# Attention with pooled keys and a phase-mixing layer: GpSimd's queue issues weight loads and a part of the other transfers

## The chip, the cores and the metric

One core of a Trainium2 chip runs the whole program. The time is device microseconds of one execution. TensorE (PE) multiplies, VectorE (DVE), ScalarE (ACT) and GpSimd (POOL) do the elementwise work, and SyncE (SP) does nothing but issue transfers between the memory of the chip and the core's on-chip memory. Every engine works through its own list of instructions in order and waits for the others by semaphores. The kernel before takes 245.79 us, the median of three runs (245.34 to 246.45).

## What is computed

```python
def _attn_ref(q, k, v):                       # (8, 8, 576, 64) each
    q_d, k_d, v_d = means over 4 neighbouring positions
    out_d = softmax(q_d @ k_d.T / 8) @ v_d
    out_up = np.repeat(out_d, 4, axis=2)
    mask = np.abs(pos[:, None] - pos[None, :]) < 4
    out_local = softmax(where(mask, q @ k.T / 8, -1e9)) @ v
    return out_up + out_local

def _moe_ref(x, w_theta, w_tok_r, w_tok_i, w_ch):   # x (8, 576, 512)
    theta = x @ w_theta
    zr, zi = x * np.cos(theta), x * np.sin(theta)
    y = einsum('ts,bsd->btd', w_tok_r, zr) + einsum('ts,bsd->btd', w_tok_i, zi)
    u = x + y
    return u + np.maximum(u @ w_ch, 0.0)
```

All inputs and the output are float32. The heads of the attention's result, side by side, are the 512 columns of x. w_theta and w_ch are 512 x 512, the two token weights 576 x 576.

## The kernel before, in words

The work goes batch by batch, 0 to 7, with several batches in flight. For a batch, 13 items are loaded in float32 into staging buffers (`st`, 15 of them, used in turn): four of k, four of q (each 128 rows of 2,304 bytes, one transfer) and five of v (two transfers each, L220, with a run of 256 bytes for each position and head). A cast to bfloat16 follows on POOL, ACT or DVE (`cast`, L226). PE turns k and q into columns (L300) through PSUM, copies bring them to kT and qT, DVE sums groups of four keys (L317) and POOL, for all batches but the first, groups of four queries (L334, L335). PE computes the pooled scores (L382, L394), the pooled v (L348, L350) and the pooled result (L414, L420), and the local scores (L468) and outputs (L500). The two parts meet in xT (L540, L552).

The second layer takes the phases (L567, L585), sine and cosine on ACT (L574, L575, L592, L593), the products z on DVE (L634), the mix over positions (L654, against WT), the sum u (L663), the channel product (L693, L699) and the relu with the residual (L706), whose left side comes turned by transposing transfers (L670). Stores go out at L719 and L725.

The weights come in 20 pieces, WITEMS: four of w_theta (128 x 512), twelve of the token weights (96 x 576; three pieces of r, three of i for the first half of the positions, then the same for the second), four of w_ch. Each goes over a staging buffer (`weight_loads`, L249) and a cast (`weight_casts`, L258) to wth, w_tm or wch; w_tm is then turned by PE (L276) into WT. The two halves of WT are read by different mixes: batch 0 takes its four mixes of the first half before those of the second.

What stands in which place is written out. ORDER is a string in which each letter is one step of a sequence (the table at L747): L one load, l one weight load, c one weight cast, C one cast of an input, J one mix, D one store, Y the two stores of a tail, 1 and 2 a load of an ACT table for sine or exponential, and so on. The kernel takes the letters one by one, and `pin` (L733) ties every instruction to the one before it on the same engine, so that the string fixes the order on each engine, SP's list of transfers too. BANKS gives the PSUM bank of each step, ENGINES the engine (v DVE, a ACT, p POOL) of each copy. In the kernel before, all 205 loads and stores and all 52 transposing transfers are issued by SP; POOL issues none.

Of the kernel before, what the change touches and what calls it, by code (L numbers as in the profile page):

```python
# [14 lines left out]
P = 128  # L15
# [3 lines left out]
D = 64  # L19
DM = 512  # L20
# [14 lines left out]
WR = 9  # L35
PG = CH // 4
KP = 32
HALF = 64
# [3 lines left out]
OC = 96  # L42
# [3 lines left out]
def kernel(  # L46
# [11 lines left out]
    nc = tc.nc  # L58
# [5 lines left out]


    ORDER = (
        "kLCLkLkCk2ACLCkaAkLCkLLCLLLCdlCaAAaaSkLkklSLLedSLLePsLCmsCOOmLkLsPpCCLlCookipULOuuxxLoCCOCNiioCCcN1l"
        "nLinTAAnnQcaClcaATLCmqtacCtOAHdTaoiSlhLXLdtyTeleLLsSPtsHPlCCmOpcLpSCsmloCTiOCcUlOtocuXuHoiOhcCiVhxom"
        "xNyiCGccHLALLganLVvVnLZVvLzNVlvVlXClvvLCnVnyCAQlvValhCACCveVLqXcvTtTcaAvlTtyaOoticHdTS2STsLsdecJHcJV"
        "LhcXttJvVhyVCVCvvvlXVyvLGVCVLVLgJLvZCvLVvvPjjjpCmJUjLuuHOxjoCiCOPJpxomiLNCXnHjLJnChNjAcLCJnyhCnLXjyT"  # L70
        "azCQLAAJCqaAlTLlLdJtLaSaLCjtOsoOiceJjjoCSLmLCJcTiClOtjsLCSCUHCRJeCuoiTTudRsCxLLjACtLJhaLtALJaGjmgOOj"
        "xPoJRoCiHiCcSpPjedCCXRKsLpmbyhKNZACnXbLHyaCLHhnXKyCLNhLLAbXzfKLCamUnSnyCuLfOJojCLiQRuCJJbAdsCLjJTmqR"
        "SjaOtjJCoseTAixxCatPPjpRLKdRDALLKJbCpSmbCOasToiNLtADnJLLjCnaNLLOnSHoiTLCjCJLnTtsOLjhotRCOCCLHXTiQohG"
        "HygDXiHThLmqhLCXZytztAKyTCabHODhLOteoLUumHDoiuiXRKhyRCfOCSbSJTsRoiLJsLdjCxADajtJejLPOpPLmopJxTDdtXjN"
        "JnnyDRjGJXCgNjHJmhniACHnaCCKjZLyLLCCbXQAChTdqRCKXyabKJySb2sLUjuKOzeutLSoesmCbCLCLSiJTmDJDjsCOPCjRpPo"
        "iJRLpOtjOoOoixHLioxTCChJiNAatnDJCHjDRndNALTLhKTtHnabnCtXeKQOjJyCoRbjGiTXgKhLHqKAFmhfLRZbJXbajyXAzJCy"
        "TyjtOaSJsoTiDtECjOromSUJuetTiKSRDsDstdOHjJJbHuxojTjJmthRiDPOYMOjhxJpJofiOomjiMOFjPoJpNiMjRNDnHnnofTn"
        "KKQbDhiGqEKTKbMtgHZRbyrzTKRhDTtYTyytbyHttKHDFJEGJhMjgbHjJDHhJMMjJrJZbMhDjyyjJzhDjRjyJjyKJJRJRKJYbJjD"
        "RKJjRjbjfRbJjDJjKjKjKKKfDREKbbRKDDbFDbbbrDDDYbD"
    )  # L80
    BANKS = (
        "0246024602467406240652064102456042605201650216452014601246012540160254602367012045106450164067340626"
        "4502610542612046025045620154062706420654205672065476025764205645074206742074620634062047016420176451"
        "0462107426107642076425062450215420346534203675204670246230463046230461346023026743126317430143064132"
        "604524360467253640234602043201450346751047236054176370101054231067542350167"
    )
    ENGINES = dict(
        C=(
            "vapaaaaavpvvappppppapppvpapppppppppppppvapvpappvappapppppppavpvapappaapppaaaaapppppaaaapapppappp"
            "appaavaa"  # L90
        ),
        a="avaavaaaavaaaaaaaaaaaaaaaaaaaaaa",
        c="aapapppappppppppappp",
        f="ppvpapap",
        q="vaaavvva",
        u="vavvavavaaaaaaaa",
        v="vvvvaaaavvvvaavaaa",
    )


# [23 lines left out]
    engines = {s: iter(e) for s, e in ENGINES.items()}  # L124

    def copy(step, **operands):
        copies[next(engines[step])](**operands)  # L127

    def tile_of(name, shape, dt=BF16):
        return const.tile(shape, dt, name=name)
# [80 lines left out]
    def load(b):  # L213
        for it in ITEMS:
            c = int(it[1])
            if it[0] == "v":
                t = stage((b, it))[:, 0:DM].rearrange("p (h d) -> p h d", d=D)
                for g in range(2):
                    lo = W0[2 * c + g]
                    nc.sync.dma_start(out=t[W * g:W * g + W], in_=v[b, :, lo:lo + W, :].rearrange("h p d -> p h d"))  # L220
            else:
                src = k if it[0] == "k" else q
                nc.sync.dma_start(out=stage((b, it)), in_=src[b, 2 * c:2 * c + 2].rearrange("h (p r) d -> (h p) (r d)", r=WR))
            yield

    def cast(b):  # L226
# [4 lines left out]
        for it in ITEMS:  # L231
# [3 lines left out]
            else:  # L235
# [6 lines left out]
    wth = tile_of("wth", [P, 4, DM])  # L242
    wch = tile_of("wch", [P, 4, DM])
    WT = tile_of("WT", [P, 9, S])
    w_tm = [rot("uT", [P, 6, S], BF16, 2) for _ in range(2)]
    WITEMS = ([("th", i, 0) for i in range(4)] + [("tok", ri, ct) for hf in range(2) for ri in range(2) for ct in range(3 * hf, 3 * hf + 3)]
              + [("ch", i, 0) for i in range(4)])

    def weight_loads():  # L249
        for kind, i, ct in WITEMS:  # L250
            t = stage((kind, i, ct))
            if kind == "tok":
                nc.sync.dma_start(out=t[0:OC], in_=(moe_w_tok_r, moe_w_tok_i)[i][OC * ct:OC * ct + OC, :])
            else:
                nc.sync.dma_start(out=t[:, 0:DM], in_=(moe_w_theta if kind == "th" else moe_w_ch)[P * i:P * i + P, :])  # L255
            yield

    def weight_casts():  # L258
        for kind, i, ct in WITEMS:
            t = staged.pop((kind, i, ct))  # L260
            if kind == "tok":
                copy("c", out=w_tm[i][0:OC, ct, :], in_=t[0:OC])
            else:
                copy("c", out=(wth if kind == "th" else wch)[:, i, :], in_=t[:, 0:DM])
            yield

    held = {}
# [434 lines left out]
    osbs = {}  # L702
# [13 lines left out]

    def store(b):
        for c, cols in channel_pieces(b):
            nc.sync.dma_start(out=out[b, P * c:P * c + P, cols], in_=osbs.pop((b, c, cols.start)))  # L719
            yield  # L720

    def tail_store(i):
        osb = osbs.pop(("t", i))
        for e in range(2):
            nc.sync.dma_start(out=out[2 * i + e, 512:576, :], in_=osb[HALF * e:HALF * e + HALF])  # L725
        yield


# [18 lines left out]
    sequences = {  # L747
        "k": constants(), "1": table(AF.Sin), "2": table(AF.Exp),
        "L": each(load), "C": each(cast), "l": weight_loads(), "c": weight_casts(), "V": weight_turns(), "v": weight_turns_out(),
        "A": each(turns), "a": each(turns_out), "d": each(key_sums), "e": each(query_sums),  # L750
        "U": each(pooled_v), "u": each(pooled_v_out), "x": each(pooled_v_last),
        "P": each(pooled_scores), "p": each(pooled_exp), "N": each(pooled_out), "n": each(pooled_norm),
# [48 lines left out]
```

## Time and profile before

The profiled execution took 245.89 us; the span of its instructions is 244.2 us, and 1.7 us lie around it. Times below are microseconds from the span's start.

| | before |
|---|---|
| median of three runs | 245.79 us |
| profiled execution, its span | 245.89 us, 244.2 us |
| granted PE clock, mean | 0.979 (half from 39.7 to 46.5 us) |
| first turn on PE (L300) | 5.18 us |
| first mix (L654) | 55.34 us |
| last mix ends | 232.05 us |
| last theta, token and w_ch weight issued | 22.4, 55.3, 80.4 us |
| from issue to landing, median: k, q, v | 4.8, 5.3, 5.1 us |
| ACT_TABLE_LOAD on ACT | 22 of 1.283 us |
| read and written in the chip's memory | 34.11 MB, 9.44 MB |

A busy time is the time of an engine's instructions; issuing a transfer does not count as busy. An idle time is put down to what ended it, the releaser. SPq in a row is SP's queue issuing. A stage's row gives for each engine the busy time and, in brackets, the number of instructions.

### The profile page before, as it was taken

What the parts mean: (1) busy time and instruction counts of PE and PEld (TensorE: products, weight loads), DVE (VectorE), ACT (ScalarE), POOL (GpSimd) and SP (SyncE); (2) the same over time, 40 slices, a digit from 0 to 9 for tenths busy, and PEclk for the clock granted to TensorE, in tenths of its full rate; (3) what the DMA queues carried; (4) which work ended last, traced back from release to release, by engine and by line L of the source; (5) the groups of instructions that cost most, each with busy time, mean ns of one, the idle gap of its engine ahead of it and who ended that gap; (6) DMA issues with size and microseconds to landing.
All of it is one profiled execution on the core that took longest, in us unless ns stands there. A gap on an engine that the chain in (4) does not pass through costs nothing.

```text
span 244.2 us, 8224 instructions
## 1 busy us (share of the span) xinstructions
PE 214.8 (88%) x3344; PEld 151.8 (62%) x3344; DVE 191.3 (78%) x393; ACT 164.9 (68%) x240; POOL 95.0 (39%) x170
## 2 busy tenths in 40 slices
PE   1466586998999999799999999999999999999990
PEld 1354453776678685487775786676676765667740
DVE  3596977797789879779799988897798978585453
ACT  3786497699799899798899859866677653420000
POOL 1785585776574594272056115923021000000000
PEclk9999997799999999999999999999999999999997
DMA  6999989989999999999899989997531586966577
GB/s 203 280 211 295 278 179 241 312 206 189 263 299 227 280 273 149 194 267 268 194 244 271 146 240 262 283 217 161 99 124 51 136 124 159 173 170 154 59 230 229
DMA packets 87671, 50.91 MB, mean 208 GB/s; under 512 B 72529, under 2 KB 72785, under 8 KB 87633
## 3 DMA queue, kind: packets, MB, share of 16 engines
q1 hardware_dynamic: 87632, 50.38, 91.7%
q8 instruction: 26, 0.43, 0.8%
q14 instruction: 13, 0.10, 0.2%
HBM read 34.11 MB, written 9.44 MB: 178 GB/s over the span
## 4 chain that ended last, share of the span: by engine, by line
PE 47%; DMA 22%; DVE 13%; SPq 7%; POOL 3%; issue 3%; ACT 3%; DVEq 0%; ACTq 0%; POOLq 0%
PE space L654 18%; DMA st<-in_v_dram 10%; PE space L567 7%; PE space L693 6%; DMA st<-in_q_dram 5%; SPq L220 4%; PE space L300 3%; DVE osb L706 2%; PE space L500 2%; DMA st<-in_moe_w_tok_i_dram 2%; PE space L540 2%; SPq L255 2%; DVE z L634 2%; DMA ur<-uT 1%; SPq L628 1%
## 5 line engine op out<-in xcount | busy, mean ns | idle before, releaser
L654 PE MATMUL space<-WT,z 128*128 128x288 bf16 x576 | 79.4, 286 | 0.8 <-DVE uT L663 0.4
L654 PEld LDWEIGHTS <-z 128*128 128x128 bf16 x576 | 54.0, 98 | 17.1 <-issue 1.3
L663 DVE TENSOR_TENSOR uT<-space,xT 128x288 bf16<-128x288 f32 x64 | 28.1, 449 | 11.5 <-PE space L654 9.6
L567 PE MATMUL space<-wth,xT 128*128 128x512 bf16 x128 | 33.8, 389 | 0.1
L693 PE MATMUL space<-wch,uT 128*128 128x512 bf16 (+1 forms) x132 | 31.9, 373 | 0.0
L706 DVE SCALAR_TENSOR_TENSOR osb<-space,ur 128x512 f32<-128x512 f32 (+1 forms) x33 | 21.7, 666 | 10.1 <-DMA ur<-uT 6.4
L574 ACT ACTIVATE cs<-space,pihc 128x512 bf16<-128x512 f32 x32 | 22.2, 693 | 7.9 <-issue 3.9
L520 DVE TENSOR_TENSOR tmp<-space,rl 128x512 bf16<-128x512 f32 x40 | 26.7, 679 | 0.5
L552 DVE TENSOR_TENSOR xT<-space,xdT 128x464 bf16<-128x464 f32 (+1 forms) x40 | 24.7, 627 | 1.7 <-PE space L540 1.4
L317 DVE TENSOR_REDUCE kd<-kT 128x290 bf16<-128x1160 bf16 x16 | 21.6, 1353 | 2.8 <-ACT kT L127 2.8
L480 ACT ACTIVATE pm<-space 128x1024 bf16<-128x1024 f32 (+1 forms) x24 | 20.6, 882 | 3.6 <-PE space L468 3.4
L334 POOL TENSOR_TENSOR two<-qT 128x576 f32<-128x576 bf16 x14 | 16.2, 1157 | 15.6 <-ACT qT L127 8.6
L127 POOL CAST q_tm<-st 128x576 bf16<-128x576 f32 x23 | 15.6, 685 | 15.6 <-DMA st<-in_q_dram 15.2
L127 POOL CAST k_tm<-st 128x576 bf16<-128x576 f32 x20 | 13.9, 700 | 18.8 <-DMA st<-in_k_dram 17.7
L127 POOL COPY ut<-uT 128x256 bf16<-128x256 bf16 x5 | 2.3, 451 | 44.5 <-DVE uT L663 44.5
L127 POOL CAST v_w<-st 128x512 bf16<-128x512 f32 x16 | 10.0, 634 | 23.9 <-DMA st<-in_v_dram 21.8
L575 ACT ACTIVATE cs<-space 128x512 bf16<-128x512 f32 x32 | 19.1, 598 | 0.0
L127 ACT COPY qT<-space 128x1152 bf16<-128x1152 bf16 x14 | 15.7, 1120 | 4.8 <-PE space L300 4.7
L693 PEld LDWEIGHTS <-uT 128*128 128x128 bf16 x132 | 12.1, 98 | 10.6 <-issue 0.3
L127 ACT COPY kT<-space 128x1152 bf16<-128x1152 bf16 x15 | 17.0, 1132 | 2.3 <-PE space L300 1.9
L567 PEld LDWEIGHTS <-xT 128*128 128x128 bf16 x128 | 11.5, 100 | 10.2 <-issue 0.8
L300 PE MATMUL space<-ident,k_tm 128*128 128x128 bf16 x144 | 12.1, 236 | 6.4 <-ACT k_tm L127 6.1
(95 smaller groups left out, 397.1 us busy)
## 6 DMA issues: line engine op xcount, KB each, us to landing
st<-in_v_dram SPq DMA_DIRECT2D x80, 128.0 KB, 5.1
st<-in_k_dram SPq DMA_DIRECT2D x32, 288.0 KB, 4.8
st<-in_q_dram SPq DMA_DIRECT2D x32, 288.0 KB, 5.3
out_dram<-osb SPq DMA_DIRECT2D x31, 256.0 KB, 3.3
st<-in_moe_w_tok_r_dram SPq DMA_DIRECT2D x6, 216.0 KB, 5.1
st<-in_moe_w_tok_i_dram SPq DMA_DIRECT2D x6, 216.0 KB, 4.8
out_dram<-osb SPq DMA_DIRECT2D x10, 128.0 KB, 2.5
st<-in_moe_w_theta_dram SPq DMA_DIRECT2D x4, 256.0 KB, 6.3
```

The costliest lines, as they stand in the source:

```text
L127: copies[next(engines[step])](**operands)
L300: nc.tensor.transpose(out=ps[:, P * r:P * r + P], in_=(k_tm if what == "k" else q_tm)[:, i, r, :, :], identity=ident)
L317: nc.vector.tensor_reduce(out=kd[:, hs, :, 0:PG].rearrange("p e g m -> p (e g) m"), axis=AX.X, op=ALU.add, in_=kT[:, hs, :].rearrange("p e ...
L480: nc.scalar.activation(out=pm.rearrange("p e c j w -> p e (c j w)"), in_=held.pop(("S", b, u))[:, :, 0:4 * W * n], func=AF.Exp, scale=SCL)
L520: nc.vector.tensor_tensor(out=tmp.rearrange("p g (j d) -> p g j d", d=D), in0=held.pop(("loc", b, c))[:, :, :, 0:D], in1=rls.pop((b, c)).u ...
L552: nc.vector.tensor_tensor(out=xT[:, :, CH * c:CH * c + cnt].rearrange("p e (m j) -> p e m j", j=4), in0=held.pop(("xT", b, c))[:, :, 0:cnt ...
L567: nc.tensor.matmul(out=th, lhsT=xT[:, dc, P * c:P * c + P], rhs=wth[:, dc, :], start=(dc == 0), stop=(dc == 3))
L574: nc.scalar.activation(out=cs[:, 0, :], in_=th, func=AF.Sin, bias=pihc, scale=1.0)
L654: nc.tensor.matmul(out=ps, lhsT=z[:, j, P * dc:P * dc + P], rhs=WT[:, j, 288 * hf:288 * hf + 288], start=(j == 0), stop=(j == 8))
L663: nc.vector.tensor_tensor(out=uT[:, dc, cols], in0=held.pop(("u", b, dc, hf)), in1=xT[:, dc, cols], op=ALU.add)
L693: nc.tensor.matmul(out=ps, lhsT=uT[:, dc, P * c:P * c + P], rhs=wch[:, dc, cols], start=(dc == 0), stop=(dc == 3))
L706: nc.vector.scalar_tensor_tensor(out=osb, in0=ps, scalar=0.0, in1=rest, op0=ALU.max, op1=ALU.add)
```

## The change

Weight loads are issued by POOL's queue, and go from float32 in the chip's memory to bfloat16 in wth, w_tm and wch in one transfer, with no staging buffer; `weight_casts`, its letter c and its engines are gone. A new function `move` takes the queue of a transfer from ENGINES, s for SP and p for POOL: the loads of q and k (L: 20 on SP, 44 on POOL), the stores of the batches (D: 16 on SP, 17 on POOL) and those of the tails (Y: 3 on SP, 5 on POOL). Loads of v and the transposing transfers stay with SP. ORDER, BANKS and the engines of the copies are new throughout. The number of casts of inputs on POOL goes from 59 to 52 (ACT 34 to 38, DVE 11 to 14); the letters 1 and 2, four before, are two.

```diff
     ORDER = (
+        "LkkkkkkL2LLLCCACLkLLLkaLCAkCLLaCCldACeCAaLCLaCCdeLLSSskSLksPmCspOomLPLLUlLlOpuiOkLLCuLoLoCxOoixNLinN"
+        "lilAnCCCLlCCanLAlCAmCLanaQdAqCTTLTetaeTtLCOtdSsSoCtHiPCsmLPUTuptpuOOohmolHxiLhXHOlxCliCGoyNgCLXinyHh"
+        "NOnShnoCnVsQXTiqLACCvlyACatVVTVLXvvVtvvAalVCVVvlAZvvmTlaHVayvltSlSsCeOCoLzLLHiLLTVdJsTvLLhtLVtXevLhV"
+        "JCVvVCCvHvyCLLHVGLLVhdvVvgUChvVJuluXjvAjJLSZjaP2jCxLzxPCyCLLCJXppLsyCjmlAaCNXnyCJRLAACjnJLeCaCaNLdJS"
...
     )
...
     ENGINES = dict(
...
+        D="sppppppspssssppppssspsspppppsssss",
+        L="sppppsppspspspppppspspssppppppppppspppppppsppspspppspspspssppssp",
+        Y="pspspspp",
...
+    queues = dict(s=nc.sync, p=nc.gpsimd)
+
+    def move(step, **operands):
+        queues[next(engines[step])].dma_start(**operands)
...
                 src = k if it[0] == "k" else q
-                nc.sync.dma_start(out=stage((b, it)), in_=src[b, 2 * c:2 * c + 2].rearrange("h (p r) d -> (h p) (r d)", r=WR))
+                move("L", out=stage((b, it)), in_=src[b, 2 * c:2 * c + 2].rearrange("h (p r) d -> (h p) (r d)", r=WR))
...
     def weight_loads():
         for kind, i, ct in WITEMS:
-            t = stage((kind, i, ct))
             if kind == "tok":
-                nc.sync.dma_start(out=t[0:OC], in_=(moe_w_tok_r, moe_w_tok_i)[i][OC * ct:OC * ct + OC, :])
+                nc.gpsimd.dma_start(out=w_tm[i][0:OC, ct, :], in_=(moe_w_tok_r, moe_w_tok_i)[i][OC * ct:OC * ct + OC, :])
             else:
-                nc.sync.dma_start(out=t[:, 0:DM], in_=(moe_w_theta if kind == "th" else moe_w_ch)[P * i:P * i + P, :])
-            yield
-
-    def weight_casts():
-        for kind, i, ct in WITEMS:
-            t = staged.pop((kind, i, ct))
-            if kind == "tok":
-                copy("c", out=w_tm[i][0:OC, ct, :], in_=t[0:OC])
-            else:
-                copy("c", out=(wth if kind == "th" else wch)[:, i, :], in_=t[:, 0:DM])
+                nc.gpsimd.dma_start(out=(wth if kind == "th" else wch)[:, i, :],
+                                    in_=(moe_w_theta if kind == "th" else moe_w_ch)[P * i:P * i + P, :])
             yield
...
         for c, cols in channel_pieces(b):
-            nc.sync.dma_start(out=out[b, P * c:P * c + P, cols], in_=osbs.pop((b, c, cols.start)))
+            move("D", out=out[b, P * c:P * c + P, cols], in_=osbs.pop((b, c, cols.start)))
...
         for e in range(2):
-            nc.sync.dma_start(out=out[2 * i + e, 512:576, :], in_=osb[HALF * e:HALF * e + HALF])
+            move("Y", out=out[2 * i + e, 512:576, :], in_=osb[HALF * e:HALF * e + HALF])
```

The lines of ORDER shown are the first four of the new thirteen; they hold the first 400 steps. POOL's transfers among the first steps are, in order: k1, q0, q1, k2, q2 and q3 of batch 0, the first piece of w_theta, then k1, q1, k3 and q2 of batch 1, and so on; SP issues k0, k3 and all of v of batch 0, then k0, q0, k2 and v of batch 1.

More of the change, by code (lines that the diff above doesn't have):

```diff
@@ L66 @@
     ORDER = (
[L67 to L76, printed above, removed]
@@ L77 @@
-        "TyjtOaSJsoTiDtECjOromSUJuetTiKSRDsDstdOHjJJbHuxojTjJmthRiDPOYMOjhxJpJofiOomjiMOFjPoJpNiMjRNDnHnnofTn"
-        "KKQbDhiGqEKTKbMtgHZRbyrzTKRhDTtYTyytbyHttKHDFJEGJhMjgbHjJDHhJMMjJrJZbMhDjyyjJzhDjRjyJjyKJJRJRKJYbJjD"
-        "RKJjRjbjfRbJjDJjKjKjKKKfDREKbbRKDDbFDbbbrDDDYbD"
+        "LkkkkkkL2LLLCCACLkLLLkaLCAkCLLaCCldACeCAaLCLaCCdeLLSSskSLksPmCspOomLPLLUlLlOpuiOkLLCuLoLoCxOoixNLinN"
+        "lilAnCCCLlCCanLAlCAmCLanaQdAqCTTLTetaeTtLCOtdSsSoCtHiPCsmLPUTuptpuOOohmolHxiLhXHOlxCliCGoyNgCLXinyHh"
@@ new lines @@
+        "NOnShnoCnVsQXTiqLACCvlyACatVVTVLXvvVtvvAalVCVVvlAZvvmTlaHVayvltSlSsCeOCoLzLLHiLLTVdJsTvLLhtLVtXevLhV"
+        "JCVvVCCvHvyCLLHVGLLVhdvVvgUChvVJuluXjvAjJLSZjaP2jCxLzxPCyCLLCJXppLsyCjmlAaCNXnyCJRLAACjnJLeCaCaNLdJS"
+        "jnnmjOCOooJQsRiiOLjLoCSqfiCOTJsLodACTitjJalUSCuTmJtsuOjePtjopCARHmilCOaxPJoTCpxiCTLtthNALLCLLCRjCLHa"
+        "XRmGJNynndhKLmLjgAHbCnCnCLXaHUOLChCRhLLuuKLZoyAaLzJiOSOLbeCKjXoxiLCsoJCRyXxKiSLjbAQsLbymeqJJRLdjPOaP"
+        "LjCppKLLTLCdTJLDAoaCiAjJtbTSCLtCTDjJLTCatCtCOjOtosCSKLoiHCsNmNihGHhbnmXnLAKaLnJnJdCbQymgLjeLLOjOoAqL"
@@ new lines @@
+        "CoZiCJaTCCiOOXjTDtRoHityTfCTLLCHCXCtotThXHChDyHihURAuyzthHaAXhRKGaeJHguyOPRbjSJhofiXLKJdysLCLDLXCJDm"
+        "jDxyJxjpFbSCjOPjUseoeRXZELuiJCduKyrmCRpjNnNJSbnnjPCnJjxKsQbOxzpoiqOPpKTCAaDtboJRARijmTLaJAtTtfjDNRJa"
+        "SnSnCOjYsLTCHotNTshitKnKXJGnDgLybjAmHabJLZKOOhdoXoFmRCCJyidJHjHhhKQbCXjXiqTCRjJyzSyOejTJDttDojsTJibj"
+        "SROUtoJTseiDuuJtjmTJKxjxjtORPPpopmJibRjSOMOoioiHKsNnMnNMnHnRhmbJhODOTJMoDjQjHqTtoiiGKhTEtgyTytbHKfZR"
+        "KthzyyDHbhTKHJJtJDjMfMGbDhjMJKHDrMbFgJHJDyyhRjZhjRJEzjjjDKKDbJyYyRJJbjRJJJjjRJjJjjfbrJDDKKDjKjRRKYjR"
@@ L80 @@
+        "bbfKbKbDbDDFEbKDrDKbbDDDY"
     )
     BANKS = (
[L82 to L85, printed above, removed]
+        "0246024602456024602460762340620634506435026430462301426701456015201562406745723657357210371072640267"
@@ L86 @@
+        "0274065240625406254067230540625604230623456302453061204621045062410642106724702167402674201647123460"
+        "2346012345102345163420367420674570126401230164026101426046504627052604524014672054621016756402360434"
+        "260352467320463406234067406237236745017650321657132045320167214524367541023"
     )
@@ L88 @@
         C=(
-            "vapaaaaavpvvappppppapppvpapppppppppppppvapvpappvappapppppppavpvapappaapppaaaaapppppaaaapapppappp"
-            "appaavaa"
-        ),
[L92 to L97, printed above, removed]
+            "vaavavavvaaavaaaaaapppvapppppppppppppvppaapvppapapppaapppppppappvvaapaavpppaappppaapppaappaavaap"
+            "pppapaav"
+        ),
+        D="sppppppspssssppppspssspsppppsssss",
+        L="sppppsppspspspppppspspssppppppppppspppppppsppspspppspspspssppssp",
+        Y="pspspspp",
+        a="aaaaaaaaaavavaaaavaaaaaaaavvaaaa",
+        f="vpvppavp",
+        q="vvaaavav",
+        u="avvavvaavvvvavvv",
+        v="vavvvaaaaavvvvavva",
     )
@@ L748 @@
         "k": constants(), "1": table(AF.Sin), "2": table(AF.Exp),
-        "L": each(load), "C": each(cast), "l": weight_loads(), "c": weight_casts(), "V": weight_turns(), "v": weight_turns_out(),
+        "L": each(load), "C": each(cast), "l": weight_loads(), "V": weight_turns(), "v": weight_turns_out(),
         "A": each(turns), "a": each(turns_out), "d": each(key_sums), "e": each(query_sums),
```

## The prediction

> **What bounds the kernel now.** The page comes first, then the stages, the waits, and the order of time around the places that the change touches.
>
> ```profile
> span 244.2 us, 8224 instructions
> PE 214.8 (88%) x3344; PEld 151.8 (62%) x3344; DVE 191.3 (78%) x393; ACT 164.9 (68%) x240; POOL 95.0 (39%) x170
> ...
> q1 hardware_dynamic: 87632, 50.38, 91.7%
> ```
>
> PE is busy 214.8 of 244.2 us, so 29.4 us are all that a schedule could win. POOL is busy 39%: it looks as if it had room. All transfers go through one queue of SP, and their packets fill 91.7% of the DMA engines' span.
>
> ```profile
> 0.00:10.00 10.00, 2.26 (x18) 1.76 (x18) 3.06 (x27) 4.49 (x7) 3.66 (x19) 1.00 0.83 255
> 10.00:20.00 10.00, 6.67 (x158) 4.37 (x159) 9.09 (x14) 7.00 (x9) 7.59 (x31) 1.00 1.12 199
> 20.00:30.00 10.00, 6.38 (x115) 5.46 (x114) 8.38 (x16) 6.55 (x10) 5.66 (x10) 1.00 1.07 309
> 30.00:40.00 10.00, 6.64 (x173) 4.27 (x174) 8.14 (x15) 7.94 (x11) 7.54 (x11) 0.97 0.93 198
> ...
> 50.00:60.00 10.00, 9.77 (x184) 7.49 (x181) 8.99 (x14) 9.94 (x15) 7.16 (x10) 1.00 0.95 211
> 60.00:70.00 10.00, 8.61 (x155) 6.02 (x153) 6.91 (x18) 7.86 (x15) 5.84 (x10) 1.00 0.97 289
> ```
>
> The columns are stage and length, busy PE, PEld, DVE, ACT and POOL (with counts), granted clock, DMA share and GB/s. PE misses 18 us before 40 us; the other stages from 70 to 230 us show 9.5 to 10.0 of 10. So PE's list sets the end from about 50 us on: **what makes an early input late moves the end by as much, and nothing later can win much**. In these same early stages POOL is not at 39% but busy 5.7 to 7.6 of 10, and the DMA share is 0.93 to 1.12: the engines have no room for more bytes per us.
>
> ```profile
> POOL v_w L127 <- DMA st<-in_v_dram: 21.8, 6, 6.3
> POOL k_tm L127 <- DMA st<-in_k_dram: 17.7, 7, 10.6
> POOL q_tm L127 <- DMA st<-in_q_dram: 15.2, 8, 5.1
> ```
>
> POOL idles mainly because it waits for the data that it casts. These gaps are what the new DMAs on it would have to fit into.
>
> ```profile
> 59.80 0.57 SPq L255 DMA_DIRECT2D st<-in_moe_w_ch_dram  x1
> 60.46 1.27 SPq L220 DMA_DIRECT2D st<-in_v_dram  x2
> ...
> 65.81 0.61 POOL L127 CAST v_w<-st 128x512 bf16<-128x512 f32 x1 [1.98 <-DMA st<-in_v_dram]
> ...
> 65.89 0.40 PE L348 MATMUL space<-v_w,pu 128*32 128x512 bf16 x4
> 66.47 0.24 PE L350 MATMUL space<-v_w,pu 128*32 128x128 bf16 x4 [0.19 <-POOL v_w L127]
> ```
>
> This is the place I weigh below: PE sums the pooled v of batch 2 at 65.9 us, and waits there for a POOL cast that ended at 66.4. There is no slack between POOL and PE at this point.
>
> **The parts of the change.** *Removed:* the 20 casts of the weights (L262, L264), 15 on POOL and 5 on ACT. From the rows, 11 x 0.66 + 4 x 0.61 = 9.7 us off POOL and 3.2 off ACT. The engine strings also take 7 casts of inputs (7 x 0.66 = 4.6 us) and a tail copy (0.45) off POOL, together 14.8 us. Off SP go 20 weight loads, 44 of the 64 loads of q and k, and 22 stores; at 0.38 to 0.58 us for an issue this is about 39 us of SP's queue. It had not set the pace of the early stages alone: loads land 4.8 to 5.3 us (medians) after issue though the first k took 2.95, so a backlog stands at the DMA engines.
>
> The Trainium skill (DMA: Bandwidth & Descriptors, Issuing engines are not separate DMA queues) says that DMAs started by different engines share the same 16 DMA engines, so a second issuer saves only issue time. The shares of 0.93 to 1.12 agree; by that rule alone the change would bring nothing at the start.
>
> *Also moved by the new order:* ACT's list changes between sine and exponential 12 times and not 22. The trace has 22 ACT_TABLE_LOADs of 1.283 us, so ACT saves 10 x 1.283 = 12.8 us. DVE takes over 14 small jobs (three casts, two kT or qT copies of 1.35 us, six of vd and last, one of WT, two tail copies), some 9 us on 191. Neither engine ends last in the stages that are late, except through the inputs below; I cost both at nothing, covered by PE's 9.5 to 10.0 of 10. If DVE had no room (9.8 of 10 at 120 to 130 us) the loss would be up to a few us.
>
> *Added:* 86 DMAs on POOL's queue: 20 weights, 44 loads, 22 stores. **No transfer of this trace is issued by POOL, so the price x of one has to be bounded.** From below: SP's issue of a transfer of 96 or 128 rows, 0.38 us. From above: POOL's dearest instruction, two<-qT with two operands, 1.157 us. POOL works on the list itself, so its own rows are nearer than SP's; between its cast (0.67) and that two-operand sum (1.16) I take the middle, **0.9 us**.
>
> The Trainium skill (DMA: Bandwidth & Descriptors, Latency and other measured facts) has about 1 us to the first byte for a DMA from GpSimd, against 0.6 from SP. With x = 1.0 the sum below would be 5.6 us instead of 1.9, so 251.4 us; no run so far can tell.
>
> **The sum.** I read POOL's new list from the order string, letter by letter, and add row durations. Up to the cast of v4 of batch 2 (the last that the pooled sum of batch 2 needs) it holds: start 1.4 (ident ends at 1.37), the band and pu constants 10.4, ten q or k casts x 0.67 = 6.7, seven v casts x 0.62 = 4.3, four pairs of query sums x 1.83 = 7.3, four vd products x 0.64 = 2.6: 32.7 us. Between them stand 37 DMAs (16 weights, 21 loads). So this cast ends at 32.7 + 37x: 66.0 us at x = 0.9, 46.8 at 0.38, 75.6 at 1.16, if POOL never waits.
>
> When does PE want it? I add PE's new list in the same way (a mix 1.15, a phase 0.9, a turn 0.55, a score 0.6, a transpose back 0.35 and so on): the work ahead of this sum is 41.6 against 44.4, 2.8 less, which at 0.9 of busy time is 2.5 us earlier: 65.9 - 2.5 = 63.4 us. **Late by 66.0 - 63.4 = 2.6 us.** Queued behind it on PE are the mixes of batch 0, then everything.
>
> The steps are priced by the rows of the chain of waits. The same sum at the other early places, for x = 0.9: the last token weight of the first half is issued by 44.4 and lands about 5 later, 49.4, where the old cast ended at 45.3; the old turns needed 5.6 us from there, the first mix would follow at 49.4 + 5.6 + 0.4 for the copy = 55.4 against 55.3, a loss of 0.1 to 0.2. The last one of the second half: 54.5 + 5 = 59.5 against 61.3, no loss. Cast of k0 of batch 3: 66.7 against 65.2, within the 2.6. v4 of batch 3: 81.5 against 82. v3 of batch 4: 96.8 against 96.4, also within. So PE shifts once, by 2.6 + 0.2. The first turn at 5.18 moves to about 5.5 (k1's issue ends at 2.3, 2.5 us to land as for the first k, 0.7 of cast); PE idles 7.7 of the first 10 us anyway.
>
> At the end: from the last mix (232.05) to 244.2 us there are 12.1 us; the new order leaves three channel products of batch 6 behind the last mix and not two, so it comes one product of 0.87 us earlier, and the stores of batch 6 leave SP's queue: -0.9.
>
> Sum: +2.6 + 0.2 - 0.9 = +1.9 us on the profiled execution's own 245.89 us (span 244.2, 1.7 around it), which is 0.1 over the median of 245.79: **247.7 us**. By the bounds of x: at 1.16, 75.6 - 63.4 = 12.2 late, +11.5 or 257.3; at 0.38 POOL is 16 us early, and the DMA share sets the pace (first rival).
>
> **The rivals.**
> *POOL is cheap, and the start gets better: 242.3 us (240 to 244.5).* The point is 32.7 + 37x = 63.4, x = 0.83; below it POOL is not late. For it: the weights no longer wait for a cast, so PE's waits of 1.2 us for POOL's uT, 1.4 for POOL's v_w and 2.9 for ACT's v_w (an ACT that loads ten tables less) can go. Half of these 5.5 us is 2.7, with 0.9 at the end 3.6. I take half because of what speaks against it: the DMA share leaves the data itself hardly earlier.
>
> *The issue meets DVE: 255 us.* If a POOL issue cannot write its list while DVE holds what both use, it waits for the rest of an instruction: DVE is busy 0.8 of the time with 191.3 / 393 = 0.49 us each, so 0.8 x 0.24 = 0.2 more, x = 1.1: 32.7 + 37 x 1.1 = 73.4, late by 10.0, with + 0.2 - 0.9 it is +9.3. For it: some POOL casts of 0.66 took 0.88 to 1.17 us. Against it: most took 0.66.
> That the lock exists, for copies in a fast mode, is in the Trainium skill (SBUF — State Buffer, The "DVE blocks DMA" trap); no run here has shown it on a transfer.
>
> *It is all hidden: 244.9 us.* The early stages wait for DMA engines, whoever issues; POOL's gaps (23 us idle before 66) take the issues, only the -0.9 remains.
>
> **Numbers.** Chances: forecast (246.5 to 252) 0.40, cheap POOL 0.37, meets DVE 0.13, hidden 0.10. A measurement of this kernel can tell 0.5% (1.2 us) from no change. Cheap POOL gives 0.37 of faster and the hidden case's low side 0.02: 0.39. Same: the rest of hidden, 0.08, and the forecast's low edge, 0.03. Slower: 0.50. The range goes from the cheap case, 240, to x = 1.16, 257 rounded; the forecast's own is 246.5 to 252.
>
> **What would show it.** POOL without idle time from 10 to 66 us, the cast of v4 of batch 2 later than 63.4, and PE's wait there of 2 to 3 us; the median distance between POOL's issues near 0.9 us; the tail from the last mix no longer than 12.1; 12 table loads. Issues under 0.8 us apart, POOL waiting for data, and a first mix before 55 us would make it wrong on the fast side; gaps over 1.1 us, on the slow one. A half-clock stretch (40 to 46 us before, 3.4 us of PE) at another place could add or take as much.

## The result and the profile after

The changed kernel takes **268.94 us**, the median of four runs (265.97 to 270.67), against 245.74 us for the kernel before, measured beside it: a ratio of 1.09, with a 95% interval of 1.081 to 1.099. It is slower by about 23 us. The forecast was 247.7 us with a range of 240 to 257: the direction held, the size lies far outside. The profiled span is 267.3 us at a mean granted clock of 0.945 (244.2 us and 0.979 before).

The page of the changed kernel; its columns are those of the page before.

```profile
span 267.3 us, 8138 instructions
...
PE 218.2 (82%) x3317; PEld 155.1 (58%) x3344; DVE 200.2 (75%) x407; ACT 147.3 (55%) x217; POOL 124.5 (47%) x233
...
q1 hardware_dynamic: 75952, 27.54, 53.5%
q0 software_dynamic: 7616, 20.47, 32.0%
...
PE 49%; DMA 25%; SPq 6%; DVE 6%; POOL 5%; issue 4%; ACT 2%; POOLq 0%; DVEq 0%; ACTq 0%
```

In these rows an issue on POOL does count as busy, unlike one on SP: the 86 issues are 47.1 of POOL's 124.5 us.

Of the 23.1 us of span, PE's busy time accounts for 3.4 (218.2 against 214.8, from stretches at a lower clock); the other 19.7 are idle PE, 49.1 us where it was 29.4. The page lacks 27 of PE's 3,344 matmul records, so that some 3 us of the idle time may be work (an estimate from two runs of one kernel further down: 211.9 us with 3,314 records, 214.7 with all). There is a new queue, q0, that is POOL's. The chain that sets the end ran over transfers before as well; what grew in it are the loads of v. Its shares by engine before, and by line before and after:

```profile
PE 47%; DMA 22%; DVE 13%; SPq 7%; POOL 3%; issue 3%; ACT 3%; DVEq 0%; ACTq 0%; POOLq 0%
PE space L654 18%; DMA st<-in_v_dram 10%; PE space L567 7%; PE space L693 6%; DMA st<-in_q_dram 5%; SPq L220 4%; PE space L300 3%; DVE osb L706 2%; PE space L500 2%; DMA st<-in_moe_w_tok_i_dram 2%; PE space L540 2%; SPq L255 2%; DVE z L634 2%; DMA ur<-uT 1%; SPq L628 1%
...
PE space L652 18%; DMA st<-in_v_dram 18%; PE space L565 8%; PE space L691 6%; SPq L227 6%; DMA st<-in_q_dram 3%; PE space L298 3%; PE space L538 2%; DMA ur<-uT 2%; PE space L498 2%; DMA utr<-ut 2%; PE space L617 2%; DVE osb L704 1%; ACT pm L478 1%; PE space L466 1%
```

Transfers are 22% of 244.2 us and then 25% of 267.3, 54 and 67 us; those of v alone are 24 and 48. The bytes of the chip's memory are what they were (read and written are the same). So no bytes were added; they come in another order, and in other packets, as will be seen.

Where PE is idle is in the stages (columns: busy PE, PEld, DVE, ACT, POOL, clock, DMA share, GB/s):

```profile
0.00:10.00 10.00, 1.14 (x9) 0.88 (x9) 2.84 (x27) 3.73 (x5) 8.37 (x31) 1.00 0.82 226
...
30.00:40.00 10.00, 3.92 (x116) 2.63 (x114) 6.13 (x11) 4.14 (x5) 4.83 (x7) 0.82 1.07 209
...
60.00:70.00 10.00, 6.03 (x81) 4.13 (x80) 5.74 (x14) 7.35 (x14) 4.62 (x8) 1.00 1.08 241
80.00:90.00 10.00, 7.72 (x185) 5.98 (x183) 8.19 (x18) 5.16 (x7) 6.77 (x12) 0.88 1.15 210
...
120.00:130.00 10.00, 5.39 (x91) 4.22 (x80) 3.88 (x7) 4.88 (x7) 1.63 (x3) 0.93 1.21 196
```

This is not one shift: PE loses 1 to 5 us in a stage, again and again (before, it was busy 2.3, 6.6, 8.6, 9.9 and 10.0 in these five). From 30 us on POOL is busy only 1.6 to 6.8 of 10 in them, so it is not POOL that is full, while the DMA share is 1.07 to 1.21: the engines wait for transfers. Which one, the chain in order of time says (start, length, what), here its four longest pieces before 130 us:

```profile
27.12 10.68 DMA st<-in_v_dram
...
58.83 9.42 DMA st<-in_v_dram
...
89.54 9.52 DMA st<-in_v_dram
...
112.72 10.98 DMA st<-in_v_dram
```

All four are v, 9.4 to 11 us from issue to use (the next longest is a load of q, 8.17 us); v's median landing is 7.3 us (5.1 before). In SP's own queue one sees the same from the other side (columns: start, length, instruction):

```profile
0.81 0.86 SPq L134 DMA_DIRECT2D st<-in_k_dram  x2
1.71 13.87 SPq L227 DMA_DIRECT2D st<-in_v_dram  x10
...
18.17 18.49 SPq L227 DMA_DIRECT2D st<-in_v_dram  x10
```

An issue of v alone takes 0.63 us; ten take 13.87 and 18.49 us: SP's queue is stopped behind transfers that do not get on. Last, the place that the prediction had weighed, POOL's list and PE's at the pooled sum of batch 2:

```profile
57.33 1.13 POOL L134 DMA_DIRECT2D st<-in_k_dram  x2
58.43 1.09 POOL L134 DMA_DIRECT2D st<-in_q_dram  x2
59.49 0.56 POOL L134 DMA_DIRECT2D st<-in_k_dram  x1
...
62.47 0.63 POOL L129 CAST v_w<-st 128x512 bf16<-128x512 f32 x1
68.40 0.62 POOL L129 CAST v_w<-st 128x512 bf16<-128x512 f32 x1 [5.30 <-DMA st<-in_v_dram]
...
69.07 0.24 PE L348 MATMUL space<-v_w,pu 128*32 128x128 bf16 x4 [2.20 <-POOL v_w L129]
```

PE does wait 2.20 us for POOL's cast, but POOL had been idle 5.30 us before it, for v. A POOL issue takes 0.55 us, and POOL was ready at 63.1.

Ratios below are against the kernel before, run beside each. Some executions of a kernel are a little longer than their fellows: the ratios leave these out (but for the run that casts loads in the new order, where all four stand in it), so that two medians, 249.53 and 247.39, are above what the ratio says, and the profiles of four runs in the old order (the 44 loads alone, the late loads, the stores, the cast loads) are of such executions.

### The profile page after: what moved, and what is told of

Its sections match the earlier page's. It is cut to its first block, busy times and chain, and to the rows that moved or that the text cites. A ratio compares the mean times of both kernels' runs of the same rounds, so it can differ in the third digit from the quotient of the medians.

```text
span 267.3 us, 8138 instructions
## 1 busy us (share of the span) xinstructions
PE 218.2 (82%) x3317; PEld 155.1 (58%) x3344; DVE 200.2 (75%) x407; ACT 147.3 (55%) x217; POOL 124.5 (47%) x233
## 4 chain that ended last, share of the span: by engine, by line
PE 49%; DMA 25%; SPq 6%; DVE 6%; POOL 5%; issue 4%; ACT 2%; POOLq 0%; DVEq 0%; ACTq 0%
PE space L652 18%; DMA st<-in_v_dram 18%; PE space L565 8%; PE space L691 6%; SPq L227 6%; DMA st<-in_q_dram 3%; PE space L298 3%; PE space L538 2%; DMA ur<-uT 2%; PE space L498 2%; DMA utr<-ut 2%; PE space L617 2%; DVE osb L704 1%; ACT pm L478 1%; PE space L466 1%
## 5 line engine op out<-in xcount | busy, mean ns | idle before, releaser
L652 PE MATMUL space<-WT,z 128*128 128x288 bf16 x576 | 81.9, 293 | 0.0
L652 PEld LDWEIGHTS <-z 128*128 128x128 bf16 x576 | 55.7, 100 | 16.5 <-issue 0.4
L134 POOL DMA_DIRECT2D out_dram<-osb x22 | 12.1, 551 | 43.1 <-DVE osb L704 43.0
L691 PE MATMUL space<-wch,uT 128*128 128x512 bf16 (+1 forms) x121 | 30.9, 372 | 0.5
L129 POOL CAST v_w<-st 128x512 bf16<-128x512 f32 x20 | 12.7, 639 | 36.5 <-DMA st<-in_v_dram 30.7
L361 POOL TENSOR_TENSOR vd<-last,own 128x256 bf16<-128x256 bf16 x16 | 10.0, 642 | 29.9 <-DVE last L129 24.1
L486 DVE TENSOR_TENSOR pm<-pm,band 128x1024 bf16<-128x1024 bf16 (+1 forms) x24 | 18.3, 764 | 5.2 <-ACT pm L478 5.2
L538 PE MATMUL space<-ident,tmp 128*128 128x116 bf16 (+1 forms) x160 | 14.8, 223 | 6.9 <-DVE osb L704 6.6
L298 PE MATMUL space<-ident,k_tm 128*128 128x128 bf16 x144 | 13.5, 253 | 6.9 <-ACT k_tm L129 6.9
L129 ACT COPY kT<-space 128x1152 bf16<-128x1152 bf16 x13 | 14.6, 1119 | 8.2 <-PE space L298 8.2
```

What stands on the lines that cost most here:

```text
L298: nc.tensor.transpose(out=ps[:, P * r:P * r + P], in_=(k_tm if what == "k" else q_tm)[:, i, r, :, :], identity=ident)
L652: nc.tensor.matmul(out=ps, lhsT=z[:, j, P * dc:P * dc + P], rhs=WT[:, j, 288 * hf:288 * hf + 288], start=(j == 0), stop=(j == 8))
L691: nc.tensor.matmul(out=ps, lhsT=uT[:, dc, P * c:P * c + P], rhs=wch[:, dc, cols], start=(dc == 0), stop=(dc == 3))
```

## The experiments

Three theories. **S**: with two queues the DMA engines take a packet of one, then of the other; POOL's packets are long, v's on SP are short, so v starves. **O**: the new order itself is worse. **W**: transfers that cast are dear.

### The loads, then the stores, back to SP

```diff
-        L="sppppsppspspspppppspspssppppppppppspppppppsppspspppspspspssppssp",
+        L="ssssssssssssssssssssssssssssssssssssssssssssssssssssssssssssssss",
```

> The kernel after with all 64 loads of q and k issued by SP; weights (with the cast) and 22 stores stay with POOL. Theory S (shares): while both queues have a backlog each DMA engine takes a packet of one and a packet of the other in turn; POOL's carry 4,608 bytes and hold an engine 214 ns, SP's packets of v 256 bytes and 18 ns, so v comes too late, and SP, stuck in its issues of v, makes the transposes late. Then this run gets most of the loss back: 244 to 252 us, and v lands in a median of 5 to 5.7 us (7.3 after). Theory O (order): the new order itself puts v and what SP waits for too late, on whatever queue: 262 us or more.

Measured: 251.83 us, ratio 1.028 (1.017 to 1.039), v lands in 5.3 us (median). The 44 loads on POOL's queue cost 17 us of the 23; the rest stays with the new order.

In the second run the D and Y strings are all s as well, and only the weights are POOL's.

> The kernel after with the loads of q and k and all stores issued by SP; only the 20 weight loads stay with POOL. S: as e1 within 3 us (stores come late, when the loads are done), 244 to 253. O: 262 or more. If the stores on POOL cost something of their own, this run is faster than e1 by over 1%.

Measured: 251.95 us, 1.028 (1.018 to 1.038), v 5.1 us. In this order it makes no difference who issues the stores. What is left over the kernel before, 6 us, is in the chain of this run:

```profile
75.17 4.27 DMA st<-in_q_dram
...
86.01 6.37 DMA st<-in_v_dram
...
94.70 4.26 DMA st<-in_k_dram
```

Inputs come late here too, one after another from the one queue: PE is busy 6.42 of 10 in the stage from 90 us, where the same weights in the old order (the next run) leave it 9.68. Against that run the first mix starts 2.4 us later (55.1 against 52.7), the last mix ends 9.8 us later (236.4 against 226.6), and from there to the end it is 14.9 us and not 11.2.

### The old order with only the weights on POOL

The 20 weight loads go through POOL with the cast on the way, the weight casts and their letter are gone; all else is the kernel before.

> The kernel before with the order before; only the weight loads go to POOL's queue with the cast on the way, and the 20 casts fall away. S: a small loss, the 20 transfers take their turns against v only in the first 80 us: 245 to 251, v lands in 5.1 to 5.8. O: 243 to 246, since the order is the old one. A theory W, that a transfer with a cast is dear for the DMA engines, wants over 250.

Measured: **238.98 us, 0.975 (0.967 to 0.984)**, faster than both kernels and below what any of the three theories gave. A second time, on another chip:

> The old order with only the weights cast on the way by POOL's queue, a second time, on the chip of these runs and beside them: 238 to 240.5 us. It is the measure for the run with the stores on POOL as well (244.58 us): if this one comes to 243 us or more, that loss was the chip and not the stores.

Measured: 240.13 us, 0.976 (0.970 to 0.982). Its stages:

```profile
20.00:40.00 20.00, 15.44 (x313) 11.28 (x310) 16.59 (x32) 13.45 (x17) 15.68 (x29) 0.89 1.15 256
40.00:60.00 20.00, 19.35 (x333) 14.62 (x331) 17.36 (x35) 17.86 (x31) 14.88 (x24) 0.94 0.88 188
60.00:80.00 20.00, 19.93 (x377) 14.87 (x375) 18.00 (x39) 17.86 (x25) 10.79 (x17) 1.00 1.27 251
```

PE is busy 19.9 of 20 us from 60 us (18.5 before) and 15.4 from 20 us (13.0 before); the first mix starts at 53.06 us (55.34). Theory W falls: this part of the change is its gain, 6 to 7 us. Whether by the queue or by the casts that go:

```diff
-                nc.gpsimd.dma_start(out=w_tm[i][0:OC, ct, :], in_=(moe_w_tok_r, moe_w_tok_i)[i][OC * ct:OC * ct + OC, :])
+                nc.gpsimd.dma_start(out=t[0:OC], in_=(moe_w_tok_r, moe_w_tok_i)[i][OC * ct:OC * ct + OC, :])
```

so with staging and casts as before, on POOL's queue (the other weights likewise).

> The kernel before; the weight loads go to POOL's queue but in float32 to staging buffers, and the 20 casts stay. If e3's gain comes from the casts that fell away (on POOL and ACT, and the buffers that they held), this run is 245 to 249, as before or worse. If it comes from the queue (the weights overtake v on a queue of their own), 238 to 241.

Measured: 249.53 us, 1.009 (1.004 to 1.015). The other queue alone costs 0.9%; the gain of the run before comes from casting on the way, which frees 20 casts and 20 turns of the staging buffers; which of the two is worth more was not tried.

### The old order with the loads on POOL

The kernel before, with the 44 loads issued by POOL as in the change (`move("L", ...)`), first without the weights, then with them.

> The kernel before with the order before; 44 of the 64 loads of q and k, by the letters of the kernel after, are issued by POOL, all else as before. S: clearly slower, 252 to 270, v lands in 6.5 us or more. O: 244 to 248, v in 5 to 5.5.

Measured: 261.54 us, 1.063 (1.049 to 1.076); v lands in 5.5 us, below the 6.5 expected of theory S.

> The kernel before with the order before; the weight loads with the cast and 44 of the loads of q and k go to POOL. If the costs of the parts add up: e4's +15.7 us for the loads and e3's -6.9 for the weights give 252 to 257. If the loads on POOL only hurt because the weights stood on SP or the like, 239 to 245.

Measured: 259.09 us, 1.053 (1.046 to 1.060), v 6.2 us; above the 252 to 257 expected if the costs of the two parts add up. The loads cost 16 to 20 us in this order too, but here not by v alone: in the first of the two runs PE is busy 2.26 us from 10 to 20 us (6.67 before), and POOL's list in that run has:

```profile
8.54 0.66 POOL L128 CAST q_tm<-st 128x576 bf16<-128x576 f32 x1 [5.79 <-DMA st<-in_q_dram]
9.14 0.54 POOL L135 DMA_DIRECT2D st<-in_q_dram  x1
9.67 0.54 POOL L135 DMA_DIRECT2D st<-in_k_dram  x1
10.20 1.06 POOL L135 DMA_DIRECT2D st<-in_q_dram  x2
```

Four loads stand behind a cast that waits 5.79 us for its own data.

With only the 21 loads of batches 4 to 7 moved:

```diff
-        L="sppppsppspspspppppspspssppppppppppspppppppsppspspppspspspssppssp",
+        L="ssssssssssssssssssssssssssssssssppspppppppsppspspppspspspssppssp",
```

> The old order with the weights cast on the way by POOL's queue (238.98 us), and of the loads of q and k only 21 of batches 4 to 7 on POOL's queue, all of batches 0 to 3 on SP's. If moved loads cost only where PE has no reserve of loaded inputs (before about 60 us; from 60 to 220 us PE is busy 19.4 to 19.8 of 20), these cost nothing: 237 to 242 us. If each moved load costs the same wherever it stands (259.09 - 238.98 = 20 us for 44), they cost 20 x 21 / 44 = 9.6: 246 to 251 us. Theory S would have v of batches 4 to 7 land about 6 us after issue, of batches 0 to 3 about 5.

Measured: ratio 1.0003 (0.995 to 1.005), so about 245.4 us, 6 us more than without these loads; neither 237 to 242 nor quite 246 to 251. So not the early stages alone pay. v lands after 5.6 us both before and after 70 us (5.6 and 5.0 without these loads), where S had about 5 and 6. Most of the loss, 4 to 5 us of PE, is in one stage, from 80 to 100 us (PE is busy 19.62 and 18.86 of 20 there in the two runs with the weights alone):

```profile
80.00:100.00 20.00, 14.48 (x218) 10.46 (x205) 12.27 (x25) 12.76 (x17) 13.56 (x21) 0.91 1.18 206
```

```profile
84.65 1.11 POOL L134 DMA_DIRECT2D st<-in_k_dram  x2
90.80 1.22 POOL L127 CAST k_tm<-st 128x576 bf16<-128x576 f32 x1 [5.04 <-DMA st<-in_k_dram]
91.97 1.06 POOL L134 DMA_DIRECT2D st<-in_q_dram  x2
```

POOL's list (second fence) reads: two loads of k, then 5 us of waiting for a k, and only after it two loads of q. PE waits 5.4 us in this stage for ACT, and ACT 6.4 us for a q. **An engine that both casts and issues delays its loads by every wait of its casts**; SP, which only issues, has no casts to wait for. That these two late loads of q are the whole loss of the stage is read from the order, not tried by itself.

### What two queues get, by themselves

Only transfers: v on SP's queue, k and q on POOL's, then all on SP's, then k and q on ACT's; the attention and the second layer are left out.

> Nothing is computed; transfers alone, in five stages with DVE reading every buffer between them: 40 loads of v (4 batches) from SP; 32 loads of k and q from POOL; both at once, v from SP and k, q from POOL; all 72 from SP, batch by batch; v from SP and k, q from ACT. The output holds copies of v. S (the DMA engines take the two queues in turn, and POOL's packets are 18 times as long): the first stage some 26 us (80% of 200 GB/s), in the third stage v creeps while k and q run, at a third of its lone rate or less, and k and q land nearly as fast as alone; the sum of the third stage is near the fourth's (within 10%), since only the division changes. If there is no such division, v and k, q finish together or v first, and v's rate in the third stage is over half of its lone rate. If a second queue costs the engines capacity, the third stage is over 10% longer than the fourth.

Measured, from the records of single packets (my own count):

```
stage                      v packets/us   GB/s   POOL packets/us   GB/s
v and POOL's k, q, 16-30 us      90         23          74          343
the same again, 76-92 us         92         24          74          341
v alone, 40-52 us               751        192           0            0
```

v gets an eighth of its rate while POOL's queue has work, and the packets are near one to one. POOL's packets of k and q hold two rows, 4,608 bytes, and take 202 ns (median); v's hold 256 bytes and take 18 ns. One of each in turn on 16 engines is 16 / (0.202 + 0.018) = 73 per us of each, near what is counted. The Trainium skill (DMA: Bandwidth & Descriptors, Queues, rings and completion order) states that each engine alternates between queue rows packet by packet; these counts agree.

The stages ran into each other, since nothing made one queue wait for the other's last load: the first two together took 55 us (POOL's queue had work up to 37 us of them), the third 58. On SP alone, k and q were all there after 52 us, but the last ten loads of v met the next stage's loads and landed 20 us later; at the 13.8 us from batch to batch, four batches are 55 us (an estimate). So the sum of two queues is about that of one.

With k and q on ACT's queue the counts are not one to one: from 170 to 200 us v has 181 packets per us (46 GB/s) beside 113 of ACT's (2,304 bytes, 102 ns), in bursts, with stretches of 2 us in which v stands still. v is starved there too, to a quarter of its rate and not an eighth. Why this pair of queues shares otherwise was not followed.

### The same inside the changed kernel

v on POOL's queue, k and q on SP's:

> The kernel after with the roles swapped: all 80 loads of v from POOL, all 64 of k and q from SP, weights and stores as after. S: v no longer has the short packets' share on SP and SP is not stuck in issues of v, so under 262 us if POOL's issue of a load of v (512 runs of 256 bytes) takes under 0.8 us; k and q then land later than in e1. If two queues are bad whoever carries v, 265 or more.

Measured: 276.67 us, 1.126 (1.115 to 1.137). POOL now puts 16 runs of v in one packet of 4,096 bytes (220 ns), SP's packets of k and q have 2,304 bytes (104 ns): k and q now land in 8.2 and 10.6 us, and v in 7.3, no sooner than in the change. S's figure, under 262 us, failed although the issue of a load of v took 0.70 us, less than the 0.8 that it allowed. The starved side changed with the queue, and the longer packet won again; but POOL's list also grew, by 80 issues of 0.70 us for 44 of 0.55 (POOL is busy 157.3 us, 124.5 in the change), and what each of the two costs was not separated.

Then POOL's loads in two halves each, to shorten its packets:

```diff
...
+                for cols in (slice(0, 256), slice(256, S)) if queue == "p" else (slice(0, S),):
+                    queues[queue].dma_start(out=t[:, cols], in_=rows[:, cols])
```

> The kernel after, but each of POOL's 44 loads of q and k is issued as two, of columns 0 to 255 and 256 to 575 of the same rows: the same bytes in packets about half as long (4,608 bytes before) and 44 more issues of 0.55 us, 24 us more of POOL. Theory S (the DMA engines take the two queues packet by packet, so long packets of POOL starve SP's short ones): the loads of v land sooner, median 6.6 us or less against 7.3, and the time falls to 258 to 266 us, unless the 24 us of POOL eat it. Theory O (the new order itself, the way of sharing does not matter): v's landing stays within 0.3 of 7.3 and the time stays at 268 or rises by POOL's extra work.

Measured: 266.2 us, 1.085 (1.078 to 1.092), not to be told from the change's 1.09; v 7.1 us. A miss, and an instructive one: the packets did not become shorter. POOL's queue packed four rows instead of two, into 4,096 and 5,120 bytes (186 and 295 ns). The edit changed nothing of what S speaks of, so it tested nothing but 24 us more of POOL's time, which cost nothing.

A transfer that casts does have one row in a packet. So the last pair lets the 44 loads cast into the staging buffers, in the new order and in the old:

```diff
+                queue, t = next(engines["L"]), stage((b, it))
+                if queue == "p":
+                    t = staged[b, it] = t.bitcast(BF16)[:, 0:S]
+                queues[queue].dma_start(out=t, in_=src[b, 2 * c:2 * c + 2].rearrange("h (p r) d -> (h p) (r d)", r=WR))
```

> The kernel after, but POOL's 44 loads of q and k write their staging buffers in bfloat16, cast on the way; the copies to k_tm and q_tm stay, from bfloat16. Cast transfers of the weights had one row in a packet (1,152 bytes written, 107 ns) where these loads had two (4,608 bytes, 214 ns): so as many bytes are read per ns of a packet, but a turn between the two queues becomes 107 + 18 and not 214 + 18 ns. Theory S (one packet of each queue in turn): v's packets come nearly twice as often while POOL's queue has work, v lands after 6.5 us or less (7.3), and the time falls to 256 to 264 us. Theory O (the order itself, not the sharing): v's landing stays within 0.3 of 7.3 and the time within 1% of 268.9.

Measured: **256.19 us, 1.040 (1.027 to 1.052)**, four executions from 252.51 to 258.16: 12.7 us off the change, with the same order, the same queues and the same number of instructions for each load. Nor did the copies get much cheaper by reading bfloat16: 0.67 to 0.68 us on POOL and ACT (0.68 to 0.72 in the change), and only the five on DVE 0.45 and not 0.75. v lands in 6.7 us (a little above the 6.5 expected). The packets are 1,152 bytes of 107 ns, twice as many, so that POOL's queue takes the same time of the DMA engines in all; only a turn is half as long. In the stage from 60 to 65 us:

```
                    v packets/us   GB/s   POOL packets/us
the changed kernel       221         56          50
loads cast on the way    455        116          83
```

```profile
span 250.5 us, 8168 instructions
...
PE 215.0 (86%) x3344; PEld 151.6 (61%) x3344; DVE 196.9 (79%) x407; ACT 146.1 (58%) x217; POOL 125.2 (50%) x233
...
q1 hardware_dynamic: 75952, 27.54, 56.9%
q0 software_dynamic: 10432, 13.98, 33.1%
```

```profile
60.00:70.00 10.00, 9.23 (x145) 7.64 (x145) 8.63 (x17) 8.46 (x15) 8.84 (x16) 1.00 1.32 186
```

These are averages over moments with and without work in POOL's queue, so they are not one to one. In the microseconds from 59 and from 63 us, when it has most, the changed kernel shows 55 and 79 packets of v beside 53 and 67 of POOL's.

The page (first fence) has POOL's queue at 33.1% where it was 32.0% of a longer span: 1,327 against 1,369 us summed over 16 engines. The stage (second fence) has PE busy 9.23 of 10 where the change had 6.03. Theory O would have had no change here, so S is shown in the place itself, not only by itself. The starvation is not gone: v's share of the chain is 14.5% (18 in the change), and PE is busy only 5.47 and 6.99 of 10 in the stages from 30 and 110 us.

> The old order with weights and the 44 loads of q and k on POOL's queue (259.09 us, v 6.2 us), these loads cast into the staging buffers as well. Theory S: v lands after 5.7 us or less and the time falls to 248 to 256 us. If what costs there is that a load stands in POOL's list behind a cast that waits for data, the packets change nothing: 257 to 261 us.

Measured: 253.61 us, 1.027 (1.018 to 1.035), against 259.09, and v 5.7 us, as S expected: 5 to 6 of the 20 us in the old order come from the packets; the rest fits the loads standing behind POOL's waiting casts, but was not tried by itself.

### The stores on POOL in the old order

The old order with the weights on POOL, and stores by the D and Y strings of the change.

> The old order with the weights cast on the way by POOL's queue (238.98 us), and the 17 stores and 5 tail stores that the change gives to POOL issued there as well; all loads of q and k on SP. POOL is busy under 6 of 20 us from 160 us on, so its list has room: 236.5 to 241 us, no difference that can be measured. If a store that waits for the relu on DVE holds back POOL's casts of the next inputs, PE waits for a v or k of batches 4 to 6 and it is 242 us or more.

Measured: 0.996 (0.991 to 1.001), about 244.4 us, where the same without the stores has 0.976: the stores cost 5 us here. Neither reason given fits: no cast is late. DVE is (start, length, instruction; DVE's list, then POOL's of the same time):

```profile
118.87 0.68 DVE L520 TENSOR_TENSOR tmp<-space,rl 128x512 bf16<-128x512 f32 x1
119.47 2.99 DVE L488 TENSOR_TENSOR pm<-pm,band 128x512 bf16<-128x512 bf16 x1
```

```profile
118.70 0.54 POOL L136 DMA_DIRECT2D out_dram<-osb  x1
119.23 0.68 POOL L129 CAST k_tm<-st 128x576 bf16<-128x576 f32 x1
119.84 0.67 POOL L129 CAST q_tm<-st 128x576 bf16<-128x576 f32 x1
120.45 0.54 POOL L136 DMA_DIRECT2D out_dram<-osb  x1
121.00 1.16 POOL L334 TENSOR_TENSOR two<-qT 128x576 f32<-128x576 bf16 x1
122.24 0.74 POOL L335 TENSOR_TENSOR qdT<-two 128x288 bf16<-128x288 f32 x1
```

The mask product of DVE, at least 0.37 us (this shape) and 0.68 in the median of both shapes, takes 2.99: it ends at 122.46, 0.3 us after POOL's unbroken run of work ended its two-operand sum at 122.16. A second one takes 2.85 us at 151.8 in the same way. PE misses 4.5 of the 40 us from 120 to 160, where without the stores it misses 1.0, and all that it waits for there is DVE; so these two waits can account for some 3.5 of the 5 us. That POOL's unbroken list is the cause is read from the order of events, not tried by itself.

## Why the prediction was wrong

*The price of an issue, x = 0.9 us*, failed: POOL's 86 issues took 0.52 to 0.57 us, by the mean of each kind. (The 1.0 us that was tried beside it from the Trainium skill, DMA: Bandwidth & Descriptors, Latency and other measured facts, is there a time to the first byte, which need not be a time of POOL's list.) By the prediction's own sum the cast of v4 of batch 2 would then end at 32.7 + 37 x 0.55 = 53 us, POOL is not late, and the rival of the cheap POOL would have held, 242.3 us. The sum of the list itself was good: POOL's rows up to this cast, 37 transfers among them, add up to 53.1 us; the rest up to 69.0 is waiting. **So the forecast's sign was right for a wrong reason.** The cast ended at 69.0 and PE waited 2.20 us, near the 2.6 forecast, but for data: of the marks named ahead, POOL without idle time, issues 0.9 apart, the first mix near 55.4 (58.77) and the tail failed, and only the late cast, the wait of PE and the 12 table loads came as said. The first turn, put at 5.5, came at 6.86.

*The step that failed most* is the landing: each sum took about 5 us from issue to landing from the old trace, whoever issues, and the moving of loads between queues was costed at nothing because the DMA engines were full anyway. They were, and their total hardly changed; but what a second queue changes is who is served. v went from 5.1 to 7.3 us in the median and to 9 to 11 us where it counts. The rule of the Trainium skill that was weighed there (DMA: Bandwidth & Descriptors, Issuing engines are not separate DMA queues), that a second issuer saves only issue time, led the same way: it holds for the bytes (55 and 58 us on two queues against about 55 on one), and the 17 us were lost in their order. The prediction's own rows could have warned: it read a DMA share near 1 as no room for more bytes per us, but the share of 1.07 went with 309 GB/s and that of 1.12 with 199, so what fills the engines is the time of packets and not bytes.

*"PE shifts once"* failed: the starvation comes back with each batch whose k and q POOL fetches while v of the batch before is under way, so the loss is paid at 30, 60, 80, 110 and 120 us. (The statement that PE was busy 9.5 to 10.0 of 10 in all stages from 70 to 230 us before overlooked one, 8.53 from 100 us; that does not change the argument.)

*SP's 39 us of freed issue* were given no gain, and none is seen; SP became a bottleneck instead, with 18.5 us for ten issues of v.

*The tail, -0.9*: from the end of the last mix (250.1) to the end are 17.2 us, not 11.2; a mis-sized term, 6 us, of which the new order with one queue for the loads already has 3.7 (14.9). The turning transfer of the last tail took 4.61 us, and the span ends 7.9 us after POOL had issued the last store, at 259.4 (before, 2.5 us after SP's last).

*ACT's saved table loads and DVE's 14 jobs*, costed at nothing: ACT is 17.6 us less busy, and no row shows that anything came earlier for it. Right, as far as is seen.

*Part by part*, from the runs: the weights cast on the way, -7; the new order brought by one queue, +13 (238.98 to 251.95); the 44 loads on POOL's queue, +17, of which 12.7 go with shorter packets; the stores, 0 in the new order. -7 + 13 + 17 = 23 is the change. The gain that the rival of the cheap POOL saw in the weights is real, and larger than its 3.6 us (tail included). The new order itself stands in the prediction's sum only as 0.9 us gained in the tail; its 13 us are the second step that failed. Why the new order is that much worse on one queue was followed only as far as late inputs and a tail of 15 us, and not tried further, so this cause stays open.

## What to carry to other kernels

In these runs the transfers of SP's and POOL's queues shared the DMA engines by the packet and not by need: before moving a stream to a second queue, look at the packet's time on each, and keep the one with short runs, on which the next stage waits, from running beside long ones. Cast on the way where it takes away a cast and a buffer, which here is worth 2.5% by itself; and let loads that feed a pipeline be issued by an engine that does nothing else, for on another they stand behind every wait in its list. When an edit has several parts, run each alone: here one part was a gain of 7 us inside a loss of 23.

## What the runs showed of the hardware

- POOL's queue packs rows into packets: two of 2,304 bytes (4,608), four of 1,024 or 1,280 (4,096 and 5,120), 16 of 256 (4,096); a transfer that casts has one row (1,152 bytes written, 107 ns). Cutting a load in two does not shorten its packets.
- SP's and POOL's queue side by side, near one packet of each in turn: 90 and 74 packets per us, and v at 23 GB/s where it has 192 alone. SP's and ACT's: 181 and 113, and v at 46 GB/s.
- DVE's product of two on-chip operands took up to 2.99 us while POOL worked without a gap (at most 2.34 in the changed kernel, 1.14 in the kernel before, 0.97 with only the weights on POOL; median 0.68). The Trainium skill (SBUF — State Buffer, SBUF: two separate sides) says that a DVE instruction with two such operands and a POOL instruction that reads on-chip memory exclude each other for a whole instruction; the rows agree that DVE waits, and show it over four POOL instructions on end, an issue among them. The prediction's rival had this the other way round, DVE holding up POOL's issues, and 0.55 us for an issue speaks against that.
